# A gated recurrence with a highway layer: long GpSimd pieces and a new written-out order

## The chip, the cores and the metric

The kernel runs on one core of a Trainium2 chip. The metric is device time in microseconds (us) of one execution. The engines are TensorE (PE in the profile), VectorE (DVE), ScalarE (ACT), GpSimd (POOL) and SyncE (SP), whose queue issues all large DMAs here.

## The reference

Four sequences of 6,336 tokens with 256 channels pass a gated linear recurrence, and its output passes a highway layer. Cut to what is computed:

```python
sig = 1.0 / (1.0 + np.exp(-f_logit))
f = lower_bound + (1.0 - lower_bound) * sig
i = 1.0 - f
for t in range(S):                       # per sequence
    h = f[:, t] * h + i[:, t] * x[:, t]
    y[:, t] = h
x = y.reshape(B * S, D)
H = np.maximum(x @ w_h, 0.0)
T = 1.0 / (1.0 + np.exp(-(x @ w_t + b_t)))
out = T * H + (1.0 - T) * x
```

x, f_logit and the output are float32, 25,344 x 256 each, 26 MB; the kernel reads two of them and writes one.

## The kernel before, in words

The tokens are cut into 28 units (`units`): two of 256 tokens, one of 512, 23 of 1,024, one of 512 and one of 256. With P = 128 partitions, a unit of 1,024 tokens has NB = 8 blocks of 128. Every unit goes through the same steps, each a small function `do_<letter>`:

- `l`, `x`: SP loads f_logit and x of the unit (1 MB each for 1,024 tokens), each into one of six slots (L263).
- `u`: ACT takes the sigmoid of -f_logit (L275), tokens on partitions.
- `b`: u * x, in float16 x float32 to bfloat16 (L283). It is cut into quarters of 512 columns (two blocks); POOL does them, or DVE where the token ends in `v`.
- `i`, `p`: PE transposes u and b into PSUM (L289, L309), one instruction group for each half of the channels. `p` needs all quarters of its unit's b.
- `f`: the gate from the transposed u (L300 on ACT; L298 on DVE with `v`).
- `s`: the recurrence itself, `tensor_tensor_scan` on DVE (L326), one for each half; the carry ties each unit to the one before.
- `z`, `g`: the two matrix products (`ffn`, L343, and L141 for the repeated weights).
- `t`: sigmoid of z on ACT (L356). `d`: DVE, max(-(1-lower_bound) y, g), that is H - x (L360).
- `E`, `e`: the product d * t (`times`, L365), 2,048 columns for a unit of 1,024 tokens, four quarters. `E` does quarters on POOL, one of up to 512 columns at a time, up to the column that the unit's last number gives; `e` does the rest on DVE in one instruction.
- `o`: PE adds y and e, and so transposes them back (L384, L385); half a unit at a time. `c`: ACT (or DVE with `v`) copies it from PSUM (L394, L392) into one of four slots o. `w`: SP writes it (L399).

Nothing is scheduled at run time. The string `order` is the program: its tokens, read from left to right, are issued one by one, and each engine keeps that order. A token is a letter, the unit, after a dot the half or quarter, and after a colon the slot of the buffer that it fills (`b5.2:2` is quarter 2 of b of unit 5, into slot 2; `*k` adds k filling matmuls). SP's queue is in order too: a `w` that waits for its `c` keeps back the `l` and `x` behind it.

Two things tie POOL to DVE. `shared` remembers the last DVE instruction that takes two inputs from SBUF (b, e, a few at the start) and makes the next POOL instruction wait for it:

```python
        if not gpsimd:
            held[:] = [ins]
        elif held:
            tc.add_manual_dep(ins.ins, held.pop().ins.name, ...
```

And both feed the same consumers: `o` needs all quarters of e that lie in its tokens, whichever engine made them.

Of the kernel before, what the change touches and what calls it, by code (L numbers as in the profile page):

```python
# [19 lines left out]
def kernel(  # L20
# [20 lines left out]

    units = [
        (0, 128, 2, 0, 'y', 4, 512),
        (0, 128, 2, 256, 'y', 4, 512),
        (0, 128, 4, 512, 'y', 4, 1024),
        (0, 128, 8, 1024, 'y', 4, 512),
        (0, 128, 8, 2048, 'y', 4, 0),
        (0, 128, 8, 3072, 'y', 4, 2048),
        (0, 128, 8, 4096, 'y', 4, 2048),
        (0, 128, 8, 5120, 'y', 4, 0),  # L50
        (0, 128, 8, 6144, 'y', 4, 512),
        (0, 128, 8, 7168, 'y', 4, 1536),
        (0, 128, 8, 8192, 'y', 4, 512),
        (0, 128, 8, 9216, 'y', 4, 2048),
        (0, 128, 8, 10240, 'y', 4, 256),
        (0, 128, 8, 11264, 'y', 4, 2048),
        (0, 128, 8, 12288, 'y', 4, 2048),
        (0, 128, 8, 13312, 'y', 4, 1024),
        (0, 128, 8, 14336, 'y', 4, 0),
        (0, 128, 8, 15360, 'y', 4, 2048),  # L60
        (0, 128, 8, 16384, 'y', 4, 0),
        (0, 128, 8, 17408, 'y', 4, 2048),
        (0, 128, 8, 18432, 'y', 4, 1024),
        (0, 128, 8, 19456, 'y', 4, 1024),
        (0, 128, 8, 20480, 'y', 4, 2048),
        (0, 128, 8, 21504, 'y', 4, 1024),
        (0, 128, 8, 22528, 'y', 4, 1024),
        (0, 128, 8, 23552, 'y', 4, 512),
        (0, 128, 4, 24576, 'y', 4, 512),
        (0, 128, 2, 25088, 'y', 4, 0),  # L70
    ]
# [4 lines left out]
z0.1:1 d1.0:1 f3.1:3 z0.0:2 i3.0:0 d1.1 s2.0:2 p2.1:1 t0.1:0 b3.3v x5:5 t0.0 z1.1:0 s2.1 l6:1 g2.0*4:1 b3.1 b3.0v
f3.0:2 u4:2 x6:0 z1.0:2 E0.0:0 b4.2:1 b4.1 t1.0:1 b4.0 p3.1:0 t1.1 i4.1:1 b4.3 f4.1:1 o0.0:2 g2.1:0 d2.0:2 z2.1:1
s3.1:3 p3.0:1 c0.0:0 z2.0:2 w0.0 d2.1 t2.1:2 l8:2 i4.0:0 E1.0:1 t2.0 f4.0:0 x7:1 E2.1:2 E2.0 s3.0 p4.1:0 z3.1:1 u5:0
s4.1:0 p4.0:1 b5.2:2 g3.0:0 t3.1:0 s4.0 b5.1 i5.1:0 d3.0:0 u7:1 g3.1:1 f5.1:3 u6:2 i7.1:1 i5.0:0 g4.1:2 f7.1:2 d3.1
g4.0:0 o2.0:1 f5.0:1 c2.0:1 d4.1:2 b5.0 b5.3 l9:3 w2.0 p5.0:1 z3.0:2 b6.0:0 b6.3 p5.1:0 b6.2 x8:2 b6.1 t3.0 o1.0:2  # L80
z4.0:1 u8:0 d4.0 x9:3 z4.1:0 s5.0:2 s5.1 t4.0:1 i6.0:1 E3.0:0 b7.1:1 c1.0v:2 w1.0 t4.1 e3 e4:2 i6.1:0 b7.0 f6.0:0
g5.1:1 z5.0:0 p6.1:1 l10:4 f6.1:1 p6.0:0 u9:2 d5.1:1 o3.0:2 c3.0:3 o4.0:1 b7.2 g5.0:2 c4.0:0 s6.1:1 b7.3 b8.0:2 i8.1:1
w3.0 w4.0 z5.1:1 t5.0:2 o3.1:0 b8.2 f8.1:3 s6.0 d5.0 t5.1 p7.1:1 i7.0:0 c3.1:1 b9.1:0 b9.0 E5.1:1 o4.1:2 s7.1:3 g6.0:1
f7.0:1 c4.1:2 d6.0:0 p7.0:0 E5.0 i8.0:1 z6.1:0 s7.0 u10:1 z6.0:1 g6.1:2 b8.3 l12:5 f8.0:0 b8.1 E5.3 E5.2 w3.1 w4.1
i9.0:1 p8.0:0 b9.3 b9.2 d6.1 o5.1:2 s8.0:0 t6.1:0 t6.0 f9.0:2 g7.0:1 i9.1:1 E6.3:0 c5.1:3 p8.1:0 x10:4 E6.2 z7.0:0
l11:0 E6.1 d7.0:2 o5.0:2 f9.1:1 g7.1:1 u12:0 s8.1 c5.0:0 p9.1:1 d7.1 i10.1:0 t7.0:1 f10.1:0 z8.0:2 z7.1:1 b10.0:1
b10.1 g8.1:0 p9.0:0 t8.0:2 z8.1:2 t7.1 s9.1:2 d8.1:1 u11:2 g8.0:1 w5.1 i12.1:1 E6.0 t8.1 b10.2 s9.0 x11:5 b10.3
f12.1:3 o6.1:0 e7:2 x12:0 d8.0 o6.0:2 i11.1:1 w5.0 p10.1:0 b11.3:2 z9.0:1 c6.1:1 f11.1:1 e8:1 b12.3:0 i10.0:1 g9.0:0
l13:1 c6.0:2 s10.1:1 t9.0:0 b11.1 b11.0 l15:2 b12.0 z9.1:2 f10.0:2 p10.0:0 o7.1:1 w6.1 i11.0:1 t9.1 g9.1:2 c7.1:3
d9.0:0 s10.0 o7.0:1 d9.1 f11.0:0 b11.2 p11.0:0 w6.0 b12.2 u13:1 s11.0:3 E9.1:0 x13:1 z10.1:2 E9.0 c7.0:0 e9 t10.1:1  # L90
g10.1:0 w7.1 i13.1:1 d10.1:2 b12.1 p11.1:0 s11.1 u15:2 g10.0:2 E9.2 o9.1:1 o9.0:0 f13.1:2 x15:2 E8.0 l14:3 b13.0:1
i12.0:1 b13.2 c9.1:1 w7.0 b13.3 i15.1:0 z11.0:1 b15.1:2 f12.0:0 p12.0:1 d10.0 z10.0:2 c9.0:2 x14:3 t11.0:0 o8.0:0
f15.1v:1 t10.0 w9.0 p12.1:0 b13.1 o8.1:2 s12.0:2 g11.1:1 c8.0:3 s12.1 i13.0:1 u14:0 E10.0:2 z12.1:0 b15.0 w9.1 d11.1:0
p13.1:0 z11.1:1 f13.0:0 i14.1:1 c8.1:0 e10 b14.1:0 w8.0 s13.1:0 g11.0:2 b14.2 t12.1:2 t11.1 l16:4 z12.0:0 b14.3
f14.1:3 w8.1 b14.0 x16:4 g12.0:1 t12.0 i14.0:0 p13.0:1 f14.0:2 d11.0 o10.0:2 d12.0:1 o10.1:1 c10.0:2 s13.0 l17:5
g12.1:0 E11.2:0 E11.0 E11.1 i15.0:1 p14.1:0 d12.1 c10.1:1 u16:1 z13.0:2 g13.0:0 e12:1 t13.0:1 f15.0:0 s14.1:1 o11.0:1
c11.0:3 E11.3 z13.1:2 p14.0:1 b16.3:1 b15.2 t13.1 b15.3 i16.0:0 f16.0:3 o11.1:1 d13.0:2 b16.0 g13.1:2 i16.1:0 w10.1
s14.0 c11.1:0 w10.0 p15.1:1 l20:0 d13.1 u17:0 w11.0 x17:5 b16.1 E12.0 s15.1:3 f16.1:2 z14.1:1 z14.0:0 b16.2 g14.1:2
d14.1:0 p15.0:1 l19:1 w11.1 i17.1:0 t14.1:0 E13.2:2 E13.3 s15.0 o12.1:2 E13.1 t14.0 g14.0:0 l18:2 x19:0 x18:1 u20:2
o12.0:1 c12.1:1 w12.1 d14.0 E13.0 p16.0:1 z15.0:2 b17.1:0 l21:3 f17.1:1 b17.0 b17.3 c12.0:2 E14.2:0 p16.1:0 t15.0:2  # L100
b17.2 s16.0:2 o13.1:1 g15.0:0 E14.1 i17.0:1 u19:1 o13.0:2 s16.1 f17.0:0 d15.0:1 p17.0:0 s17.0:0 g16.0:0 c13.0:3
c13.1:0 p17.1:1 u18:0 z15.1:1 E14.0 z16.1:2 E14.3 d16.0:2 i19.1:0 s17.1 g16.1:0 t15.1 w12.0 w13.0 x21:3 g15.1:1 d15.1
f19.1:3 w13.1 i18.0:0 i20.0:1 b19.1:2 b19.3 t16.1:1 g17.0:2 x20:2 b18.2:1 f18.0:2 i18.1:0 o14.0:1 b18.0 d16.1 d17.0:0
b18.3 b18.1 e15:1 E15.1 g17.1:0 o14.1:2 d17.1 b19.2 E15.0 f20.0:0 f18.1:1 c14.0:1 p18.1:1 u21:0 z16.0:1 z17.0:0
s18.1:1 t16.0 p18.0:0 o15.1:1 t17.0:0 b19.0 s18.0 b21.2:0 o15.0:0 c14.1:2 p19.1:1 z17.1:2 c15.1:3 e16:2 E17.1:0
b20.1:1 c15.0:0 i19.0:0 z18.1:1 b20.0 b20.3 l22:4 t17.1 b20.2 w14.0 g18.0:0 f19.0:1 z18.0:2 w14.1 p19.0:0 s19.1:3
E17.3 i20.1:1 d18.0:1 w15.1 t18.1:2 t18.0 o16.1:1 E17.0 g18.1:2 o16.0:0 b21.1 s19.0 d18.1 f20.1:2 w15.0 p20.0:1
i21.1:0 c16.1:1 z19.0:1 c16.0:2 E17.2 f21.1:3 x22:4 g19.1:0 b21.0 u22:1 b21.3 s20.0:2 z19.1:2 p20.1:0 i22.0:1 d19.1:2
s20.1 l23:5 t19.0:1 g19.0:0 o17.0:1 i21.0:0 f22.0:1 w16.1 t19.1 e18:1 g20.1:2 c17.0:3 f21.0:0 w16.0 d19.0 p21.0:1
o17.1:1 b22.1:2 b22.3 E19.1:2 d20.1:0 u23:2 p21.1:0 E19.2 z20.0:0 s21.0:0 o18.0:2 c17.1:0 t20.0:0 b22.0 z20.1:1  # L110
i23.1:1 x23:5 s21.1 b22.2 g20.0:0 c18.0:1 t20.1 o18.1:2 f23.1:2 d20.0 l24:0 p22.0:0 c18.1:2 w17.0 s22.0:1 i22.1:1
g21.0:1 z21.1:0 f22.1:0 i23.0:1 u24:0 b23.2:1 b23.1 p22.1:0 z21.0:2 d21.0:1 t21.1:2 E19.3 s22.1 g21.1:1 b23.0 E19.0
w17.1 o19.0:0 t21.0 E20.1:0 w18.0 f23.0:3 b23.3 x24:1 d21.1 c19.0:3 l25:1 o19.1:2 p23.0:1 i24.0:0 w18.1 z22.0:1 e20
c19.1:0 s23.0:3 b24.0:0 f24.0:1 g22.1:0 g22.0:2 E20.0 i24.1:1 x25:0 d22.1:2 b24.2 t22.0:1 p23.1:0 o20.1:1 d22.0 u25:1
b24.1 z22.1:0 b24.3 w19.0 s23.1 f24.1:0 w19.1 E21.0:1 l26:2 e21 o20.0:2 b25.0:2 l27:3 c20.1:1 p24.1:1 t22.1 b25.1
g23.1:1 c20.0:2 s24.1:2 i25.0:0 b25.3 z23.0:0 f25.0:3 z23.1:2 E21.1 i25.1:0 w20.1 b25.2 p24.0:1 t23.0:0 g23.0:0 t23.1
d23.1:0 o21.0:2 E22.0:2 w20.0 o21.1:1 E22.2 f25.1:2 c21.0:3 s24.0 E22.1 p25.0:0 x27:2 d23.0 c21.1:0 z24.0:2 x26:3
E22.3 z24.1:1 u26:2 s25.0:0 g24.1:0 p25.1:1 t24.0:2 d24.1:1 s25.1 t24.1 i26.0:0 f26.0:0 o22.0:2 o22.1:1 E23.0:0
g24.0:0 i26.1:0 b26.1:1 c22.0:1 b26.0 c22.1:2 d24.0 u27:0 z25.0:2 i27.0:1 e23 e24:1 g25.0:1 f26.1:1 z25.1:0 d25.0:2
w21.0 t25.0:1 E24.0 p26.1:0 o23.0:2 f27.0:3 E24.1 p26.0:1 o24.0:1 t25.1 w22.0 g25.1:0 c23.0:3 w21.1 b27.0:0 s26.1:1  # L120
# [319 lines left out]
```

## Time and profile before

| | |
|---|---|
| three timed runs | 210.14, 210.24, 210.43 us; median 210.24 |
| span of the profiled execution, first to last instruction | 208.8 us |
| what the runs' median has beside that span | 1.4 us (the page gives no time of the execution other than its span) |
| busy: PE, DVE, ACT, POOL | 192.3, 194.4, 195.0, 171.7 us |
| moved by DMA | 78.69 MB, mean 377 GB/s |
| granted TensorE clock | 0.994 |
| b on POOL, 512 columns | 96 instructions, mean 1,179 ns |
| E on POOL, 512 columns | 54, mean 1,168 ns; one of 256 columns, 677 ns |
| e on DVE | 17, from 512 to 2,048 columns, 459 to 1,208 ns |

In the page, a busy time is the sum of the engine's instructions with overlaps counted once. On DVE, ACT and POOL the next instruction usually starts before the recorded end of the one ahead, so the distance between two starts in a dense stretch says what an instruction costs its engine, and it is shorter than the recorded duration. The rows with 40 digits cut the span into slices of 5.2 us; a digit is the busy share in tenths.

### The profile page before, as it was taken

The page shows a single profiled execution, that of the slowest core. Times are in us where ns is not written, and L with a number is a line of the kernel's source. Part 1 is how long each engine was busy: PE and PEld are TensorE (multiplying, and loading weights), DVE is VectorE, ACT ScalarE, POOL GpSimd, SP SyncE. Part 2 cuts the span into 40 slices and gives each one's busy share as a digit, 9 for nine tenths or more (in the row PEclk, how much of TensorE's full clock was granted, in tenths as well). Part 3 has the DMA queues.
Part 4 walks back from the last instruction along what each step waited for, and adds up shares of the span by engine and source line. Part 5 has one row for each costly group of instructions (what it writes and reads, how often), then busy time and mean ns, then how long its engine had stood idle before and what let it go on. Part 6 is the DMA issues. An engine that isn't in the chain of part 4 may idle for free.

```text
span 208.8 us, 4668 instructions
## 1 busy us (share of the span) xinstructions
PE 192.3 (92%) x1827; PEld 132.6 (64%) x1827; DVE 194.4 (93%) x154; ACT 195.0 (93%) x191; POOL 171.7 (82%) x162
## 2 busy tenths in 40 slices
...
DVE  0799998999999999999999999999999999999970
...
DMA  5999999999999999999999999999998999926676
GB/s 230 391 427 414 416 422 424 414 410 425 415 426 409 419 399 336 392 417 317 425 413 403 417 416 421 432 408 421 421 428 350 342 372 400 333 110 257 248 296 258
DMA packets 15982, 78.69 MB, mean 377 GB/s; under 512 B 1748, under 2 KB 2264, under 8 KB 10072
## 3 DMA queue, kind: packets, MB, share of 16 engines
...
## 4 chain that ended last, share of the span: by engine, by line
PE 44%; DMA 17%; DVE 15%; ACT 12%; issue 5%; POOL 3%; SPq 2%; ACTq 0%; DVEq 0%; POOLq 0%
DMA l<-in_f_logit_dram 13%; DVE y L326 9%; PE op L385 6%; PE z L343 6%; PE op L384 6%; PE g L343 6%; PE z L141 5%; PE bT L309 5%; PE uT L289 5%; PE g L141 5%; DVE d L360 4%; ACT f L300 4%; DMA x<-in_x_dram 4%; ACT o L394 3%; ACT u L275 2%
## 5 line engine op out<-in xcount | busy, mean ns | idle before, releaser
L283 POOL TENSOR_TENSOR bv<-u,x 128x512 bf16<-128x512 f16 x96 | 110.3, 1179 | 21.7 <-DMA x<-in_x_dram 9.6
L326 DVE TENSOR_TENSOR_SCAN y<-f,y,bT 128x1024 bf16<-128x1024 f16 (+5 forms) x54 | 106.7, 1991 | 1.1 <-ACT f L300 0.5
L365 POOL TENSOR_TENSOR e<-d,t 128x512 bf16<-128x512 bf16 (+1 forms) x55 | 62.5, 1159 | 7.6 <-DVE e L365 4.5
L360 DVE SCALAR_TENSOR_TENSOR d<-y,ncc,g 128x1024 bf16<-128x1024 bf16 (+2 forms) x56 | 63.0, 1140 | 1.1 <-PE g L343 0.9
L300 ACT ACTIVATE f<-uT,ncc 128x1024 f16<-128x1024 f16 (+2 forms) x53 | 56.4, 1073 | 3.0 <-PE uT L289 2.9
L356 ACT ACTIVATE t<-z,bt 128x1024 bf16<-128x1024 f32 (+2 forms) x56 | 57.2, 1060 | 0.6 <-PE z L141 0.2
L394 ACT COPY o<-op 128x1024 f32<-128x1024 f32 (+1 forms) x50 | 50.7, 1038 | 2.2 <-PE op L385 1.4
L275 ACT ACTIVATE u<-l 128x2048 f16<-128x2048 f32 (+2 forms) x28 | 48.8, 1748 | 2.9 <-DMA l<-in_f_logit_dram 2.9
L384 PE MATMUL op<-diag,y 128*128 128x128 f16 x396 | 49.4, 219 | 1.9 <-ACT t L356 1.3
L385 PE MATMUL op<-ident_b,e 128*128 128x128 bf16 x396 | 49.3, 219 | 0.8 <-DVE e L365 0.6
L385 PEld LDWEIGHTS <-e 128*128 128x128 bf16 x396 | 44.0, 113 | 6.4 <-issue 2.9
L384 PEld LDWEIGHTS <-y 128*128 128x128 bf16 x396 | 44.2, 113 | 2.3
L343 PE MATMUL g<-y,w_sb 128*128 128x512 bf16 (+1 forms) x112 | 39.2, 367 | 0.8 <-DVE d L360 0.4
L343 PE MATMUL z<-y,w_sb 128*128 128x512 bf16 (+1 forms) x112 | 39.0, 367 | 0.4 <-DVE d L360 0.4
L309 PE MATMUL bT<-ident_f,bv 128*128 128x128 f32 x198 | 32.0, 279 | 4.2 <-ACT f L300 2.4
L141 PE MATMUL g<-y,w_sb 128*128 128x512 bf16 x92 | 34.9, 379 | 0.0
L141 PE MATMUL z<-y,w_sb 128*128 128x512 bf16 x92 | 34.9, 379 | 0.0
L289 PEld LDWEIGHTS <-u 128*128 128x128 f16 x396 | 26.1, 98 | 12.3 <-issue 3.7
L289 PE MATMUL uT<-ident_h,u 128*128 128x128 f16 x396 | 30.6, 219 | 2.7 <-DVE y L326 2.0
L343 PEld LDWEIGHTS <-w_sb 128*128 128x128 f16 x224 | 21.8, 98 | 15.8 <-issue 0.4
L309 PEld LDWEIGHTS bT<-ident_f,bv 128*128 128x128 f32 x198 | 22.2, 141 | 12.6 <-DVE y L326 3.1
L141 PEld LDWEIGHTS <-w_sb 128*128 128x128 f16 x184 | 18.0, 98 | 16.7 <-issue 2.1
...
## 6 DMA issues: line engine op xcount, KB each, us to landing
...
l<-in_f_logit_dram SPq DMA_DIRECT2D x23, 1024.0 KB, 11.3
x<-in_x_dram SPq DMA_DIRECT2D x23, 1024.0 KB, 10.1
...
```

The source lines that it names most:

```text
L141: return pe.add_instruction(mybir.InstMatmult(name=nc.get_next_instruction_name(), start_tensor_calc=start, stop_tensor_calc=stop, tile_si ...
L283: shared(pin(e.tensor_mul(st[n]["bv"][:, k].rearrange("p d j -> p j d"), st[n]["u"][:, q:q + 2], st[n]["x"][:, q:q + 2])), not eng)
L289: pin(nc.tensor.transpose(uT[:, j * P:(j + 1) * P], st[n]["u"][:, j, h * P:(h + 1) * P], ident_h))
L300: pin(nc.scalar.activation(to, of, AF.Identity, scale=ncc[:, h:h + 1], bias=1.0))
L309: pin(nc.tensor.transpose(words[:, k:k + g * (P - 1) + 1:g], pair, ident_f))
L326: pin(nc.vector.tensor_tensor_scan(y[:, c:e], st[n]["f", h][:, c:e], st[n]["bT", h][:, c:e], 0.0 if fresh else carry[h], op0=ALU.mult, op1 ...
L343: pin(nc.tensor.matmul(p[:, a:e], w, half(n, "y", ki)[:, a:e], start=ki == 0, stop=ki == NH - 1))
L356: pin(nc.scalar.activation(half(n, "t", m), st[n]["z", m][:, :tokens(n)], AF.Sigmoid, bias=bt[:, m:m + 1]))
L360: pin(nc.vector.scalar_tensor_tensor(half(n, "d", m), half(n, "y", m), ncc[:, m:m + 1], st[n]["g", m][:, :tokens(n)], op0=ALU.mult, op1=AL ...
L365: shared(pin(eng.tensor_mul(st[n]["e"][:, a:e], st[n]["d"][:, a:e], st[n]["t"][:, a:e])), eng is nc.gpsimd)
L384: pin(nc.tensor.matmul(o, half(n, "y", h)[:, cols], diag[:, h], start=True, stop=False))
L385: pin(nc.tensor.matmul(o, half(n, "e", h)[:, cols], ident_b, start=False, stop=True))
```

## The change

The functions for b, E and e take a range of quarters instead of one: `b5.0-4` is one instruction over quarters 0 to 3 of b, 2,048 columns, and `E3.3-4` is quarter 3 of e on POOL. `e` on DVE takes a range as well. The column at which POOL's share of e ends is no longer a number of the unit, and two unused fields of a unit go. The new list gives POOL 70 quarters of e in 31 instructions (before, 54.5 in 55) and 98 quarters of b in 32 (96 in 96). DVE keeps 29 quarters of e in 11 instructions (44.5 in 17) and one quarter of b (three). Four f of 1,024 columns are on DVE (one, and one of 512); no c is on DVE (one of 512 columns). Units, buffers, slots and every other instruction are the same in kind and number; their order on each engine and the slots that they take are new.

```diff
-    units = [
-        (0, 128, 2, 0, 'y', 4, 512),
...
+    units = [
+        (0, 2), (256, 2), (512, 4), (1024, 8), (2048, 8), (3072, 8), (4096, 8), (5120, 8),
...
     order = """
+l0:0 l3:1 pc:0 wh u0:0 i0.0:0 i0.1:1 k*10 l1:2 x0:0 wt cc dg f0.1v:0 f0.0:1 x1:1 u3:1 u1:2 i1.0*5:0 WH b0.0-1v:0 l2:3
+x2:2 f1.0:2 p0.1*2:1 b1.0-1:1 i1.1:0 x3:3 l4:4 s0.1:0 p0.0:1 s0.0 f1.1:3 p1.1*2:0 p1.0:1 g0.0:1 s1.1:1 u2:0 b2.0-2:2
+i2.1:0 s1.0 i2.0:1 g1.1:0 b3.0-4:0 d0.0:0 x4:4 g1.0:2 g0.1:1 f2.1:0 d1.1:1 WTa i3.1:0 d1.0 z1.1:0 z0.0:2 f2.0:1
+p2.0*1:1 f3.1:3 t0.0:0 d0.1 z0.1:1 t0.1 p2.1:0 z1.0:2 l5:5 s2.0:2 s2.1 i3.0:1 f3.0v:2 g2.0*4:1 t1.1:1 u4:2 z2.1:0
+d2.0:2 E0.0-1:0 t2.1:2 t1.0 l7:0 p3.1:0 i4.1:1 b4.0-4:1 x5:5 o0.0:1 g2.1:0 s3.1:3 l6:1 f4.1:1 z2.0:2 c0.0:0 p3.0:1
+x6:0 w0.0 t2.0 d2.1 i4.0:0 s3.0 f4.0:0 u5:0 E1.0-1:1 u7:1 p4.1:0 p4.0:1 z3.0:1 g3.1:2 z3.1:0 s4.1:0 t3.0:0 s4.0
+E2.0-2:2 i5.0:0 t3.1 d3.1:0 g3.0:1 d3.0 f5.0:3 i5.1:1 f5.1:2 g4.0:0 u6:2 i7.1:0 o2.0:2 b5.0-4:2 p5.1:1 o1.0:1 f7.1:1
+d4.0:1 E3.3-4:0 z4.1:0 c1.0:1 l8:2 s5.1:2 t4.1:1 x7:1 c2.0:2 p5.0:0 z4.0:1 E3.0-3 i6.0:1 s5.0 t4.0 g4.1:0 g5.1:2
+i6.1:0 b6.0-4:0 x9:2 b7.3-4:1 o3.1:1 w1.0 x8:3 u8:0 f6.0v:0 i8.1:1 f6.1:2 d4.1 z5.0:0 d5.1:2 l9:3 c3.1:3 p6.0:0
+e4.0-4:2 o3.0:2 f8.1:3 p6.1:1 w2.0 o4.1:1 t5.0:2 z5.1:0 s6.0:1 s6.1 i7.0:0 l10:4 c3.0:0 c4.1:1 g5.0:2 o4.0:1 t5.1
+f7.0:0 x10:4 w4.1 b7.0-3 u9:2 p7.0:1 d5.0 g6.0:0 c4.0:2 w4.0 z6.1:2 i8.0:0 f8.0:2 s7.0:3 t6.1:0 b8.0-4:2 p7.1:1 i9.0:0
...
+f10.0:0 z9.0:2 u15:1 b11.0-4:2 p10.1:1 p10.0:0 s10.1:1 z9.1:1 t9.1:0 o7.1:0 l13:2 s10.0 g9.1:1 b12.0-4:0 w5.1 t9.0
+i11.0:1 x13:1 c7.1:1 g10.0:2 d9.1 f11.0:2 i12.0:0 o7.0:0 w6.1 d10.0:1 p11.0:1 z10.1:1 e9.0-4:1 x14:3 u13:2 s11.0:3
+f12.0:0 z10.0:2 p11.1:0 t10.1:1 s11.1 w7.1 g10.1:1 l14:3 E8.0-4:0 t10.0 i13.1:1 d10.1 c7.0:2 w6.0 o9.1:2 o9.0:0
...
+g13.0:2 t13.1:1 l19:0 t12.1 b15.0-4:0 d13.0:1 g12.0:1 i16.1:1 p14.0:0 d12.0 u17:0 s14.0 f16.1:3 z13.0:0 g13.1:2
+o11.0:1 E12.2-4:0 t13.0 e12.0-2 i16.0:1 p15.0:0 o11.1:0 d13.1 c11.0:2 o12.0:1 f16.0:2 b16.3-4:1 g14.1:2 s15.0:3
...
+i20.0:1 w13.0 i18.0:0 g17.1:1 d16.0 f20.0:2 i18.1:1 f18.0:1 o14.1:0 f18.1:0 b18.0-4:0 d15.1 g17.0:2 w13.1 w12.1
+c14.1:0 d17.1:0 p18.1:0 o14.0:1 E15.2-3 u21:0 x20:3 E15.3-4 o15.0:0 c15.0:1 b19.0-4:1 p18.0:1 d17.0 s18.1:1 w14.1
+z16.0:2 t16.0 i19.0:0 s18.0 o15.1:0 c14.0:3 e16.0-4:2 z17.0:2 x21:2 b20.0-4:2 p19.0:1 f19.0:0 c15.1:2 t17.0:0 z17.1:1
+p19.1:0 s19.0:3 o16.1:0 z18.0:2 t17.1 i20.1:1 s19.1 c16.1:0 w15.0 l22:4 g18.1:1 o16.0:0 E17.0-3:1 w14.0 d18.1:2
...
+o17.0:2 u22:1 c17.0:3 i21.0:1 b21.0-4:0 w15.1 s20.1 t18.1 x22:4 g18.0:1 g19.1:2 i22.0:0 E19.0-1:0 f21.0:3 d18.0 w16.0
+o17.1:0 d19.1 e18.1-4:2 w17.0 g20.1:1 f22.0:2 p21.0:1 c17.1:2 p21.1:0 z19.1:2 u23:2 d20.1:0 x23:5 l24:0 o18.1:0
...
+s23.1 i24.1:0 z22.0:0 f24.1:3 o20.0:2 x26:3 o20.1:1 t22.0 c20.0:1 w20.0 e21.0-4:2 i25.0:0 b25.1-2:1 p24.0:1 g23.0:0
...
+w21.0 E22.0-2:0 t24.0:2 E22.2-4 z24.1:1 d24.1:2 f26.1:2 p25.1:0 o22.0:2 o22.1:0 i27.0:1 t24.1 s25.1 E23.0-4:1 g24.0:1
+c22.0:2 f27.0:3 d24.0 c22.1:1 i26.0:1 w21.1 f26.0:0 g25.0:2 z25.0:0 z25.1:1 b26.0-2:2 d25.0:1 p26.1:0 e24.0-4:2
+o23.0:2 p26.0:1 t25.0:1 o24.0:0 b27.0-1:0 t25.1 s26.1:1 g25.1:1 w22.0 c23.0:0 E25.0-2:0 s26.0 i27.1:0 c24.0:2 f27.1:1
+w20.1 o24.1:2 p27.1:1 d25.1 c24.1:3 s27.1:2 p27.0:0 z26.1:0 w22.1 E25.3-4 o23.1:1 s27.0 t26.1:0 w23.0 c23.1:1 g26.0:2
+o25.1:0 d26.0:0 g26.1:1 z26.0:2 w24.0 w24.1 c25.1:0 t26.0 e25.2-3 d26.1 z27.0:1 e26.1-2:2 z27.1:1 o25.0:0 e26.0-1
+w23.1 t27.1:2 t27.0 c25.0:2 g27.0:0 g27.1:0 d27.1:2 o26.0:1 c26.0:3 d27.0 e27.0-1:1 w25.1 w25.0 o27.0:2 c27.0:1 w26.0
+w27.0
...
-    def do_b(n, k, eng, slot):
+    def do_b(n, k, eng, slot, end):
         if "bv" not in st[n]:
             st[n]["bv"] = sb([P, NB // 2, D, 2], BF16, "bv", slot)
-        q = 2 * k
+        blk = slice(2 * k, 2 * end)
         e = nc.vector if eng else nc.gpsimd
-        shared(pin(e.tensor_mul(st[n]["bv"][:, k].rearrange("p d j -> p j d"), st[n]["u"][:, q:q + 2],
-                                st[n]["x"][:, q:q + 2])), not eng)
+        shared(pin(e.tensor_mul(st[n]["bv"][:, k:end].rearrange("p k d j -> p k j d"),
+                                st[n]["u"][:, blk].rearrange("p (k j) d -> p k j d", j=2),
+                                st[n]["x"][:, blk].rearrange("p (k j) d -> p k j d", j=2))), not eng)
...
-    def do_E(n, k, eng, slot):
-        times(n, nc.gpsimd, k * 512, min(units[n][6], k * 512 + 512), slot)
-
-    def do_e(n, k, eng, slot):
-        times(n, nc.vector, units[n][6], NH * tokens(n), slot)
+    def do_E(n, k, eng, slot, end):
+        times(n, nc.gpsimd, k * 512, end * 512, slot)
+
+    def do_e(n, k, eng, slot, end):
+        times(n, nc.vector, k * 512, end * 512, slot)
...
         n, _, k = name[1:].partition(".")
-        here["do_" + name[0]](int(n), int(k or 0), token.endswith("v"), slot)
+        k, _, end = k.partition("-")
+        span = (int(end),) if end else ()
+        here["do_" + name[0]](int(n), int(k or 0), token.endswith("v"), slot, *span)
```

More of the change, by code (lines that the diff above doesn't have):

```diff
@@ L42 @@
     units = [
-        (0, 128, 2, 0, 'y', 4, 512),
[L44 to L66, printed above, removed]
@@ L76 @@
[L76 to L85, printed above, removed]
@@ L86 @@
[L86 to L120, printed above, removed]
@@ L121 @@
-w22.1 i27.1:0 c24.0:1 o24.1:2 s26.0 p27.0:1 f27.1:2 d25.1 w23.0 p27.1:0 E23.1 z26.1:1 s27.0:2 w24.0 E25.0:2 c24.1:0
-o23.1:0 z26.0:2 s27.1 t26.1:2 c23.1:2 z27.1:1 z27.0 e25 g26.0:1 w24.1 d26.0:1 t26.0 o25.1:0 w23.1 E26.0:1 t27.1:0
-g26.1:2 d26.1 c25.1:3 o25.0:1 w25.1 c25.0:1 g27.0:0 g27.1 e26 w25.0 d27.1:0 t27.0 o26.0:0 d27.0 c26.0:0 e27:0 o27.0:1
-w26.0 c27.0:2 w27.0
+l0:0 l3:1 pc:0 wh u0:0 i0.0:0 i0.1:1 k*10 l1:2 x0:0 wt cc dg f0.1v:0 f0.0:1 x1:1 u3:1 u1:2 i1.0*5:0 WH b0.0-1v:0 l2:3
+x2:2 f1.0:2 p0.1*2:1 b1.0-1:1 i1.1:0 x3:3 l4:4 s0.1:0 p0.0:1 s0.0 f1.1:3 p1.1*2:0 p1.0:1 g0.0:1 s1.1:1 u2:0 b2.0-2:2
@@ new lines @@
+f12.0:0 z10.0:2 p11.1:0 t10.1:1 s11.1 w7.1 g10.1:1 l14:3 E8.0-4:0 t10.0 i13.1:1 d10.1 c7.0:2 w6.0 o9.1:2 o9.0:0
+f13.1:2 c9.1:0 p12.0:1 i15.1:0 w7.0 z11.1:2 b13.0-4:1 l16:4 c9.0:1 g11.1:1 w9.0 f15.1:1 E10.0-4:2 i13.0:0 s12.0:2
+t11.1:0 f13.0:0 u14:0 p12.1:1 o8.1:0 d11.1:0 s12.1 p13.1:0 o8.0:2 w9.1 c8.0:3 c8.1:2 z11.0:1 i14.1:1 o10.0:2 t11.0
+x15:2 g11.0:0 s13.1:0 p13.0:0 l17:5 f14.1v:3 i14.0:1 d11.0 o10.1:1 s13.0 g12.1:0 u16:2 c10.0:1 b14.0-4:2 w8.1 z12.0:2
+f14.0:2 d12.1:2 i15.0:1 E11.1-4:1 p14.1:0 E11.0-1 x16:4 s14.1:1 c10.1:0 w8.0 z13.1:1 z12.1:0 t12.0:2 w10.0 f15.0:0
@@ new lines @@
+g13.0:2 t13.1:1 l19:0 t12.1 b15.0-4:0 d13.0:1 g12.0:1 i16.1:1 p14.0:0 d12.0 u17:0 s14.0 f16.1:3 z13.0:0 g13.1:2
+o11.0:1 E12.2-4:0 t13.0 e12.0-2 i16.0:1 p15.0:0 o11.1:0 d13.1 c11.0:2 o12.0:1 f16.0:2 b16.3-4:1 g14.1:2 s15.0:3
+c11.1:3 c12.0:1 u19:1 x17:5 d14.1:0 z14.1:0 p15.1:1 s15.1 z14.0:1 t14.1:0 w11.0 b16.0-3 g14.0:2 t14.0 E13.0-4:2
+i17.1:0 o12.1:0 l20:1 w12.0 p16.1:1 w11.1 f17.1:0 z15.0:1 p16.0:0 d14.0 s16.1:2 o13.0:2 c12.1:2 t15.0:2 l18:2 g15.0:0
+u20:2 s16.0 c13.0:1 i17.0:1 d15.0:2 o13.1:1 b17.0-4:2 p17.0:0 f17.0:1 z15.1:2 z16.1:0 c13.1:3 s17.0:0 E14.0-4:1
```

37 lines of the change are left out of this document (21 added, 16 removed), and 3 rows, old and new, of the table units.

## The prediction

> **What bounds the kernel now.** I read the page first, then the windows, the timelines of VectorE (DVE), ScalarE (ACT) and GpSimd (POOL), and the groups by form.
>
> The page's busy rows and slices:
>
> ```profile
> span 208.8 us, 4668 instructions
> PE 192.3 (92%) x1827; PEld 132.6 (64%) x1827; DVE 194.4 (93%) x154; ACT 195.0 (93%) x191; POOL 171.7 (82%) x162
> DVE  0799998999999999999999999999999999999970
> DMA  5999999999999999999999999999998999926676
> GB/s 230 391 427 414 416 422 424 414 410 425 415 426 409 419 399 336 392 417 317 425 413 403 417 416 421 432 408 421 421 428 350 342 372 400 333 110 257 248 296 258
> ```
>
> No engine stands out, and DMA runs near 415 GB/s until about 160 us, with dips near 80 and 96 us. The windows show who waits in the middle:
>
> ```profile
> core 0: us, PE busy (x) PEld busy (x) DVE busy (x) ACT busy (x) POOL busy (x), PEclk, DMA share, GB/s
> ...
> 120.00:140.00 20.00, 19.31 (x191) 13.64 (x189) 20.00 (x14) 20.00 (x19) 18.49 (x17) 1.00 1.01 419
> ```
>
> DVE and ACT have no free time. Durations overlap, so I priced work by start-to-start distances in dense stretches: scan y of 1,024 columns 2.26 us, d 1.17, ACT's f and t 1.00, u 1.81, o 0.90. By these, DVE has 191.6 us of work, and of its 12.1 us of idle time only 3.2 lie after its e4 at 41.2 us. ACT has 189.0 us of work and about 6.4 us of idle time between 20 us and 199 us. PE's instructions do not change, and in its timeline a 1,024-token unit takes only some 7.0 us of dense work against about 7.6 us of span (per unit: uT and bT 0.9 each, z and g 1.7 each, op 1.8), so PE gives about 15 us of room. So DVE bounds the kernel, with ACT close behind.
>
> POOL looks free at 82%, and is not. Wherever DVE does e or b (two SBUF inputs), `shared` makes the next POOL instruction wait, and the timelines (start, us, instruction) of POOL, then of DVE, show the other direction too:
>
> ```profile
> 128.55 4.56 POOL L283 TENSOR_TENSOR bv<-u,x 128x512 bf16<-128x512 f16 x4 [0.21 <-ACT f L300]
> 133.73 1.16 POOL L365 TENSOR_TENSOR e<-d,t 128x512 bf16<-128x512 bf16 x1 [0.62 <-DVE e L365]
> ```
>
> ```profile
> 132.68 0.97 DVE L365 TENSOR_TENSOR e<-d,t 128x1024 bf16<-128x1024 bf16 x1
> ...
> 169.07 0.69 DVE L365 TENSOR_TENSOR e<-d,t 128x1024 bf16<-128x1024 bf16 x1
> ```
>
> The e at 132.68 met a POOL piece that ran to 133.11 and took 0.97 us instead of 0.69: it got through only when that piece was over. So POOL and DVE's two-input work share one resource, "the port". Its work is 168.8 us (POOL) + 13.3 (e on DVE) + 1.9 (b on DVE) = 184.0 us, and from the first b at 9.9 us to E26's end at 201.7 there are 191.8 us. It is nearly as full as DVE.
>
> **The change, part by part.**
>
> *Price of a long POOL piece.* The trace has no piece over 512 columns. It has one of 256:
>
> ```profile
> L365 POOL TENSOR_TENSOR e<-d,t 128x512 bf16<-128x512 bf16 x54 | 61.8, 1168 | 7.6 <-DVE e L365 4.5 <-DVE d L360 2.4 <-DVE bv L283 0.7
> L365 POOL TENSOR_TENSOR e<-d,t 128x256 bf16<-128x256 bf16 x1 | 0.7, 677 | 0.0
> ```
>
> Start to start these are 1.115 and 0.63 us: 1.90 ns a column and 0.14 us an instruction (b's 512 takes 1.125, so 0.15). A 2,048-column piece then costs 4.03 to 4.05 us; the other end is four short pieces, 4.46 to 4.50. I take the fit, nearest to both rows, and keep the other end for a rival.
>
> The Trainium skill, "GPSIMD Engine Reference", section "Elementwise — side-by-side cycle accounting", gives 2.6 cycles an element and 4,497 ns for 2,048 fp32 columns of such an add, which is 2.2 ns a column and leaves merging nothing to save; the 256-column row (0.63 us where half of 1.115 would be 0.56) speaks against that here, for these types, and by it the sum below would come out some 13 us later.
>
> *POOL.* E goes from 54.5 to 70 quarters and b from 96 to 98: 17.5 quarters x 0.97 = +17.0 us. Instructions go from 55 to 31 (E) and 96 to 32 (b): -24 x 0.14 - 64 x 0.15 = -13.2. Together +3.8.
>
> *DVE.* e before: 4 of 2,048 columns at 1.12, one of 1,792 at 1.01, 4 of 1,536 at 0.87, 5 of 1,024 at 0.60, 3 of 512 at 0.45 = 13.3 us. After: 5, 0, 1, 1 and 4 of these = 8.9. Two b fewer: -1.3. The c on DVE goes to ACT: -0.6. f: three of 1,024 more at 1.22, one of 512 fewer at 0.66: +3.0. Sum -3.3.
>
> *ACT.* Three f of 1,024 fewer: -3.0; one f of 512 (0.57) and one c of 512 (0.56) more. Sum -1.9.
>
> *Port.* +3.8 - 4.4 - 1.3 = -1.9. PE and DMA bytes: 0.
>
> *The order.* DVE's e in the middle are fewer: e4, e9, e12, e16, e18, e21, e24 instead of thirteen from e4 to e24. By the prices above, the work that the new list puts between these meetings is, on DVE, 36.7, 27.6, 29.2, 15.0, 21.4 and 16.0 us (sum 145.9), and on the port 36.8, 27.6, 29.3, 14.5, 21.3 and 15.8 (145.3). The two go in step, with 0.1 us to spare at a meeting. In the old list, from e4 to e24, the same difference was 2.5 us over twelve steps, 0.2 each. A meeting's handshake shows as 0.2 to 0.4 us of POOL idle beyond e itself (1.27 before E11.3 for an e of 1.01). Six meetings fewer at about 0.15 that reaches DVE, against 0.1 less to spare at six: I leave DVE's idle time as it was.
>
> *The sum.* The first loads come in the same order, so x5 lands as before and POOL's b5 starts at 28.69 us. Then b5 4.05, E3.3 1.12, E3.0-3 3.06, b6 4.05, b7.3 1.13: e4 can start at 42.1, where it started at 41.2. From e4 to e27's end DVE has 155.8 us of work (before 159.3). With the 3.2 us of idle time: 42.1 + 155.8 + 3.2 = 201.1, where the trace has 203.7. From there to the end of the span 5.1 us passed (op, c27, the last write): 206.2. ACT must end 2.5 us earlier with 1.9 less work, so 0.6 of its 6.4 us of idle time must go. The last POOL piece, E25.3, ends at 42.1 + 150.8 of port work + 6 x 0.38 = 195.2, and c25.1 needs it by about 196: hidden, with under 1 us of cover. The runs last 1.4 us longer than the span (median 210.24 against 208.8): **207.7 us**.
>
> *Writes* move behind loads on SP's queue: w10.1, w6.0 and w18.0 stand several loads later. o has four slots, and a write's landing must beat the next c in its slot; the tightest in the middle is w15.0 to c16.0, 6 us, with one load ahead, where before w14.0 took 11 us to land, just when c16.1 started. No cost taken, up to 1 us if it misses.
>
> **Rivals.**
>
> *The port becomes the bound (slower).* The saving per merged start rests on one 256-column row; b has no second size at all. From b5 on 97 starts are merged away. All the cover is under 1 us, and the gain 2.6: if a merged start saves 0.11 us or less instead of 0.15, POOL is late for s and for E25.3 by the whole gain. At a third of the saving lost, 97 x 0.05 = 4.9 us, less 1 of cover: 211.6 us. At nothing saved, some 221. For it: the port has nothing to spare. Against it: the fit needs an error of 40 ns, and the 512-column distances vary by 8 ns.
>
> *DVE is held by a whole piece (slower).* Before, no piece in front of a DVE e was longer than 1.2 us, and the longest hold was 0.28. In the new list e9, e16 and e21 stand behind pieces of 4.05 us. If POOL lags before each, and DVE waits half the added length, 1.4 us, three times: 207.7 + 4.2 = 211.9. It decides from a lag of about 0.9 us at each, since 3 x 0.9 eats the gain. Against it: work between meetings is equal to 0.1 us, so a lag once paid need not come again.
>
> The Trainium skill, "SBUF — State Buffer", section "Who interferes with whom", says that the pair of ports shared by VectorE and GpSimd is an exclusive lock and that the second to issue blocks fully until the first is done; the row of 0.97 us agrees, for a hold of 0.28 us, and no run here shows one behind a 4 us piece.
>
> *DMA holds the gain back.* Between 100 and 155 us the queue is full: x18 landed at 128.39 and its b started at 128.55. The new list wants 50.9 MB landed (l21) when u21 starts, about 131.5; at the old supply, 49.3 MB by 128.39 and 415 GB/s, they are there at 132.2. If the dips at 80 and 96 us stay, about 1 us of the gain goes: 208.7.
>
> *It does nothing.* Long pieces bring what more e on POOL costs, and DVE's gain turns into waits for b: 210.2.
>
> **How the numbers follow.** Forecast 0.50, for 207.7 (its own range 206.0 to 208.6: DVE's idle time between 1.6 and 4.1 us). DMA 0.12 (208.7). Port 0.24 (from 210.7 upwards, 211.6 as its middle). Held DVE 0.08 (211.9). Nothing 0.06. This measurement tells 0.2% (0.42 us) from no change. Faster: 0.50 + 0.11 = 0.61; same 0.06 (with a little of DMA, less a little of nothing); slower 0.33. The range 206.0 to 212.0 leaves out the far half of the port case and the few hundredths below.
>
> **What would show it.** Right: POOL's 2,048-column groups at 4.03 to 4.10 us start to start, DVE work about 188.4 us, e4 at about 42.1, e27's end at about 201, DVE's e of 2,048 columns still near 1.2 us. Port wrong: those pieces at 4.2 or more, and scans y or transposes bT waiting for POOL's bv. Held DVE: single e of 2 us and more. DMA: u waiting for l between 115 and 150 us, and dips in GB/s near 80 and 96 us as before. ACT's o waiting for out_dram: the writes were moved too far.

## The result, and the profile after

Four timed runs of the changed kernel took 207.60, 207.71, 207.90 and 208.35 us, median 207.81; the kernel before, on the same chip, 210.26. The ratio is 0.988 (0.985 to 0.991): faster by 2.4 us, where 207.7 us was forecast. The profiled execution's span is 205.9 us (before 208.8), so the runs' median lies 1.9 us beyond it. Beside its own span every run on record, of either kernel, takes 1.7 to 1.9 us more; the execution on the page of before was some 0.3 us longer than the median one, whose span is 208.5. All times below are medians of all executions of a kernel; in the runs at 247.53 and 227.01 us two and one of six executions were in a slower state, and the others have medians of 246.38 and 226.85.

From the page of the kernel after, the rows shown of before:

```profile
span 205.9 us, 4570 instructions
PE 191.5 (93%) x1827; PEld 132.6 (64%) x1827; DVE 191.0 (93%) x147; ACT 192.5 (93%) x190; POOL 175.7 (85%) x74
DVE  0779999999999999999999999999999999999970
DMA  6999999999999999999999999999999997886686
GB/s 228 384 427 415 420 417 423 411 417 425 403 416 420 426 419 423 412 394 406 411 424 366 406 377 413 426 414 391 415 369 338 422 424 303 290 326 239 264 318 258
```

DVE lost 3.4 us of busy time and ACT 2.5, POOL gained 4.0. The second thing to see is in the last row: the old dips at the 16th figure (336 GB/s, about 80 us) and the 19th (317, about 96 us) are gone; the same places now show 423 and 406. Smaller ones have come at the 22nd and 24th (366 and 377).

The stretch from 120 to 140 us in the windows of after:

```profile
core 0: us, PE busy (x) PEld busy (x) DVE busy (x) ACT busy (x) POOL busy (x), PEclk, DMA share, GB/s
120.00:140.00 20.00, 19.11 (x186) 13.50 (x187) 19.73 (x13) 19.45 (x19) 18.69 (x8) 1.00 1.01 407
```

Nothing has become slack: DVE, ACT, POOL and DMA are all close to full. The groups by form of after (busy us, mean ns):

```profile
L255 POOL TENSOR_TENSOR bv<-u,x 128x2048 bf16<-128x2048 f16 x19 | 78.5, 4136 | 2.9 <-DMA x<-in_x_dram 1.6 <-DVE e L338 1.3
L338 POOL TENSOR_TENSOR e<-d,t 128x2048 bf16<-128x2048 bf16 x8 | 32.7, 4091 | 1.2 <-DVE e L338 1.2
L338 POOL TENSOR_TENSOR e<-d,t 128x512 bf16<-128x512 bf16 x12 | 13.9, 1166 | 1.5 <-PE bT L282 1.1 <-DVE d L333 0.4
L338 DVE TENSOR_TENSOR e<-d,t 128x2048 bf16<-128x2048 bf16 x5 | 6.7, 1334 | 0.0
```

A piece of 2,048 columns takes 4.1 us recorded, less than four times 1,166 ns. DVE's e of 2,048 columns has a mean of 1,334 ns where it was 1,208 before: it waits a little for POOL, as the timelines of DVE and, below, POOL show.

```profile
41.70 1.58 DVE L338 TENSOR_TENSOR e<-d,t 128x2048 bf16<-128x2048 bf16 x1
...
78.96 1.41 DVE L338 TENSOR_TENSOR e<-d,t 128x2048 bf16<-128x2048 bf16 x1
...
200.70 0.42 DVE L338 TENSOR_TENSOR e<-d,t 128x512 bf16<-128x512 bf16 x1
```

```profile
36.95 5.27 POOL L255 TENSOR_TENSOR bv<-u,x 128x2048 bf16<-128x2048 f16 x2
```

e4 starts at 41.70 but gets through only after POOL's b7.3, which ends at 36.95 + 5.27 = 42.22. The last e ends at 201.12.

### The profile page after: what moved, and what is told of

It reads as the page before. It is cut to its first block, busy times and chain, and to the rows that moved or that the text cites. A ratio compares the mean times of both kernels' runs of the same rounds, so it can differ in the third digit from the quotient of the medians.

```text
span 205.9 us, 4570 instructions
## 1 busy us (share of the span) xinstructions
PE 191.5 (93%) x1827; PEld 132.6 (64%) x1827; DVE 191.0 (93%) x147; ACT 192.5 (93%) x190; POOL 175.7 (85%) x74
## 4 chain that ended last, share of the span: by engine, by line
PE 41%; DMA 16%; ACT 15%; issue 10%; DVE 10%; POOL 5%; SPq 1%; ACTq 0%; DVEq 0%; POOLq 0%
DMA l<-in_f_logit_dram 8%; DVE y L299 6%; PE op L358 6%; PE op L357 6%; PE g L316 5%; PE bT L282 5%; PE z L316 5%; DMA x<-in_x_dram 5%; PE z L113 5%; PE g L113 5%; PE uT L262 4%; ACT o L367 4%; ACT t L329 4%; ACT f L273 4%; ACT u L247 3%
## 5 line engine op out<-in xcount | busy, mean ns | idle before, releaser
L255 POOL TENSOR_TENSOR bv<-u,x 128x2048 bf16<-128x2048 f16 (+3 forms) x32 | 102.3, 3211 | 16.8 <-DMA x<-in_x_dram 10.7
L338 POOL TENSOR_TENSOR e<-d,t 128x512 bf16<-128x512 bf16 (+3 forms) x31 | 73.6, 2391 | 2.7 <-DVE e L338 1.2
L273 ACT ACTIVATE f<-uT,ncc 128x1024 f16<-128x1024 f16 (+2 forms) x51 | 53.8, 1070 | 3.3 <-PE uT L262 3.2
L367 ACT COPY o<-op 128x1024 f32<-128x1024 f32 (+1 forms) x51 | 51.8, 1039 | 1.5 <-PE op L358 1.3
L262 PEld LDWEIGHTS <-u 128*128 128x128 f16 x396 | 26.3, 98 | 12.0 <-issue 3.8
L262 PE MATMUL uT<-ident_h,u 128*128 128x128 f16 x396 | 31.3, 220 | 2.0 <-DVE y L299 1.2
```

What stands on the lines that cost most here:

```text
L255: shared(pin(e.tensor_mul(st[n]["bv"][:, k:end].rearrange("p k d j -> p k j d"), st[n]["u"][:, blk].rearrange("p (k j) d -> p k j d", j=2) ...
L262: pin(nc.tensor.transpose(uT[:, j * P:(j + 1) * P], st[n]["u"][:, j, h * P:(h + 1) * P], ident_h))
L273: pin(nc.scalar.activation(to, of, AF.Identity, scale=ncc[:, h:h + 1], bias=1.0))
L338: shared(pin(eng.tensor_mul(st[n]["e"][:, a:e], st[n]["d"][:, a:e], st[n]["t"][:, a:e])), eng is nc.gpsimd)
```

## The theories

- P (pieces and room on the port): long pieces save about 0.145 us of port time for each start that is merged away; that room pays for the e that leave DVE.
- O (order of loads and writes): the new list gives the loads a longer lead on SP's queue, and that carries the gain, or part of it.
- Q, formed on the way: the lead carries nothing by itself, but the faster order can't run without it. SP sits at a write until its copy is made; if the loads issued ahead of it run out meanwhile, DMA stands still.

The kernel before took 210.24 to 210.37 us beside every group of runs, so the experiments are compared by their medians with after's 207.8, and with before by the ratio and its interval.

## Experiments on the pieces and the port

**The changed kernel again.**

> The changed kernel once more, beside the kernel before on the same chip, so that the others have a yardstick. Both theories: 207.6 to 208.2 us, 0.986 to 0.991 of before. P (pieces): long POOL pieces give room on the port that POOL and VectorE share, and that room lets VectorE and ScalarE give work away. O (order): the gain comes from the new order alone, above all from loads that no longer stand behind writes; the length of the pieces is by the way.

208.03 us, ratio 0.9894 (0.988 to 0.9909). So after stands at 207.8 to 208.0.

**Short pieces in the new list.** Every product on POOL is cut back to 512 columns, 168 instead of 63; nothing else changes.

```diff
-b5.0-4:2
+b5.0-1:2 b5.1-2 b5.2-3 b5.3-4
```

> The new list, but every b and E on POOL is issued in pieces of 512 columns again, one behind the other (168 instructions instead of 63). P: 105 more starts at 0.145 us are 15.2 us more on the port, of which some 14 lie behind b5 and about 1 is covered: 219 to 222 us, with VectorE's y and PE's bT waiting for bv. O: the order is the same, so 207.6 to 208.5 us.

220.48 us, ratio 1.0491 (1.0472 to 1.0509): P's figure. 12.7 us for 105 more starts are 0.12 us each. SP's order is that of after, so O alone is out. The timeline of DVE and that of POOL in this kernel (the products are at L345 and L262) show how the lost room reaches DVE:

```profile
79.10 5.49 DVE L345 TENSOR_TENSOR e<-d,t 128x2048 bf16<-128x2048 bf16 x1
```

```profile
74.46 9.05 POOL L262 TENSOR_TENSOR bv<-u,x 128x512 bf16<-128x512 f16 x8
```

POOL is late with the eight pieces that stand before e9 in the list; they end at 83.51, and DVE's product, issued at 79.10, ends at 84.59. It got in between no two of them, although three began after its own start.

**Pieces of 1,024 columns.** 97 products on POOL instead of 63.

```diff
-b5.0-4:2
+b5.0-2:2 b5.2-4
```

> After's list with POOL's pieces held to 1,024 columns: 97 POOL products instead of 63. P: a start costs 0.145 us; 34 more are 4.9 us of port work, of which under 1 us is covered: 211 to 213 us, about a third of the way to the 220.5 us that 105 more starts took. If only very short pieces cost something, or the cost is in the order: 207.6 to 209.0.

211.90 us, ratio 1.0078 (1.0065 to 1.0091): within P's range. 4.1 us for 34 starts are again 0.12 each, so the price goes with the number of starts. Where it lands is read from the groups by form of this kernel, DVE's products:

```profile
L340 DVE TENSOR_TENSOR e<-d,t 128x2048 bf16<-128x2048 bf16 x5 | 9.6, 1914 | 0.0
L340 DVE TENSOR_TENSOR e<-d,t 128x512 bf16<-128x512 bf16 x4 | 1.7, 424 | 0.2
L340 DVE TENSOR_TENSOR e<-d,t 128x1024 bf16<-128x1024 bf16 x1 | 1.6, 1599 | 0.0
L340 DVE TENSOR_TENSOR e<-d,t 128x1536 bf16<-128x1536 bf16 x1 | 1.3, 1257 | 0.0
```

Together 14.2 us; the same eleven products take 6.7 + 1.7 + 0.9 + 0.8 = 10.1 in after. So DVE's products take 4.1 us longer, waiting for the port, and the kernel loses 4.1 us. With pieces of 512 columns the same products take 19.5 us, 9.4 of the 12.7 us lost; most of the rest shows as idle time before scans.

**Merging alone.** The old list with its old shares; POOL's adjacent pieces become one (100 products on POOL instead of 151), nothing else moves.

```diff
-b4.2:1 b4.1 b4.0 b4.3
+b4.0-4:1
```

> The old list with the old shares of work, but POOL pieces that already stood next to each other are one instruction (100 instead of 151). P: 51 starts x 0.145 = 7.4 us of port time come free, but VectorE keeps 191.6 us of work and ScalarE 189.0, so only what VectorE lost at meetings can come back: 209.2 to 210.2 us. O: the old order stays, 210.0 to 210.5. A third theory, that merging alone brings the gain: 207.5 to 208.5.

211.13 us, ratio 1.0046 (1.0032 to 1.0059): a miss for every expectation. The timeline of DVE has both sides:

```profile
132.56 0.68 DVE L342 TENSOR_TENSOR e<-d,t 128x1024 bf16<-128x1024 bf16 x1
...
196.19 1.28 DVE L337 SCALAR_TENSOR_TENSOR d<-y,ncc,g 128x1024 bf16<-128x1024 bf16 x1 [0.65 <-PE g L117]
```

The hold of before is gone (0.68 us instead of 0.97), and by 191 us DVE is 0.4 us ahead. But at 196 us a d waits 0.65 us for PE, which in before it did not, and DVE ends 0.5 us behind. PE's timeline shows why it is late:

```profile
194.26 0.25 PE L362 MATMUL op<-ident_b,e 128*128 128x128 bf16 x1 [0.51 <-POOL e L342]
```

It waits for a product of 1,024 columns on POOL, from 192.07 to 194.20 us, which before came in two pieces, the first of them done by 193.6. A merged piece hands over its first columns only at its end, a price that neither the prediction nor the expectation had. Room on the port brought nothing to a list that doesn't spend it.

**Spending less of it.** E13 and E20 go back to DVE: DVE +2.3 us of work, the port -5.9.

```diff
-E13.0-4:2
+e13.0-4:2
-E20.0-4:1
+e20.0-4:1
```

> The new kernel with e of units 13 and 20 on VectorE instead of POOL, at the same places of the list: VectorE 2.3 us more work, the port 5.9 us less. If VectorE binds: 209.8 to 211.0 us (2.3, and up to 1 more where VectorE meets a piece). If the port alone binds: 206.0 to 207.8 us.

209.65 us, ratio 0.9968 (0.9958 to 0.9978). 1.6 to 1.8 us later than after for 2.3 us of work on DVE, just under the range for "DVE binds"; of the 5.9 us freed on the port at most 0.7 come back.

**Spending more of it.** The upper half of e21 goes to POOL.

```diff
-e21.0-4:2
+E21.2-4:2 e21.0-2
```

> After's list with the upper half of e21 on GpSimd (E21, 1,024 columns) and the lower half on VectorE. VectorE's work falls by 1.12 - 0.60 = 0.5 us, POOL's grows by 2.1 and the port's by 1.6. If VectorE and ScalarE bind and the port has room of 2 us and more: 207.2 to 208.0, a gain of at most 0.5. If the port is as full as the prediction had it (under 1 us of cover): 208.4 to 209.6.

208.98 us, ratio 0.9933 (0.9921 to 0.9945), 1.2 us later than after. The timeline of DVE:

```profile
173.28 0.69 DVE L338 TENSOR_TENSOR e<-d,t 128x1024 bf16<-128x1024 bf16 x1
174.50 2.35 DVE L299 TENSOR_TENSOR_SCAN y<-f,y,bT 128x1024 bf16<-128x1024 f16 x1 [0.54 <-ACT t L329]
189.78 1.95 DVE L338 TENSOR_TENSOR e<-d,t 128x2048 bf16<-128x2048 bf16 x1
```

e21 takes 0.52 us less than in after (1.21), but that is lost at once: the scan behind it waits 0.54 us and starts at 174.50, in after at 174.53; in both PE has just made a bT (at 174.41 and 174.44). Then e24 takes 1.95 us instead of 1.22, held by a POOL that is late. The port has under 1 us to spare here, as the prediction had it.

**The f shift undone.** Four f of 1,024 columns go back to ACT.

```diff
-f3.0v:2
+f3.0:2
```

(and the same for f6.0, f12.1 and f14.1)

> The new kernel with its four f of 1,024 columns on VectorE (f3.0, f6.0, f12.1, f14.1) given back to ScalarE: VectorE 4.7 us less work, ScalarE 4.0 us more. If both bound, as the prediction has it, ScalarE's 191.1 us of work end 1 to 4 us later: 208.9 to 211.9 us. If VectorE alone binds: 204 to 206.5 us.

211.01 us, ratio 1.0047 (1.0025 to 1.0069), some 3 us later than after although DVE has 4.7 us less to do. ACT binds as DVE does.

**How long POOL holds DVE.** After the kernel's work five rungs are added: a POOL product of 2,048 columns, 1, 3, 5, 7 or 9 short DVE steps of one SBUF input, then a DVE product of 512 columns with two.

> The new kernel, then five rungs at its end: a POOL piece of 2,048 columns starts together with 1, 3, 5, 7 or 9 VectorE instructions of 0.39 us that do not need the port, and then VectorE takes a product of 512 columns with two inputs from SBUF (0.42 us alone). The same product is computed again into e25, so the output stays what it is. If a held instruction waits for the whole piece: about 3.7, 2.9, 2.2, 1.4 and 0.7 us. If the port is shared between the two while both run: 0.4 to 0.9 us on each rung. The time itself is of no interest (about 250 us).

The DVE product took 3.85, 2.82, 1.79, 0.76 and 0.42 us. First and last rung in the timeline of DVE, and the first in that of POOL:

```profile
206.50 3.85 DVE L398 TENSOR_TENSOR junk<-d,t 128x512 bf16<-128x512 bf16 x1
...
247.08 0.42 DVE L398 TENSOR_TENSOR junk<-d,t 128x512 bf16<-128x512 bf16 x1
```

```profile
206.03 4.05 POOL L394 TENSOR_TENSOR e<-d,t 128x2048 bf16<-128x2048 bf16 x1 [0.59 <-DVE junk L392]
```

In four rungs DVE's product ends 0.27 to 0.29 us after POOL's, however early it began; in the fifth it begins after POOL's. POOL's takes 4.05 us in every rung. The steps took 0.52 us each where 0.39 had been expected, so the middle rungs came later than planned; the reading is the same. The Trainium skill, "SBUF — State Buffer", section "Who interferes with whom", calls these ports an exclusive lock on which the second to issue blocks fully; the 3.85 us agree, now for a whole long piece.

## Experiments on SP's queue

**Each write right behind its copy.**

```diff
-c2.0:2 ... x9:2 ... x8:3 ... l9:3 ... w2.0
+c2.0:2 w2.0 ... x9:2 ... x8:3 ... l9:3
```

(so for w2.0; all writes alike)

> The new list, but each write stands on SP's queue right behind its copy; loads that stood ahead of a late write now stand behind it. P: loads still land before they are needed for the most part, 207.6 to 208.6 us. O: loads come late again and DMA shows dips as in the old list, 209.5 to 210.5 us.

231.35 us, ratio 1.0994 (1.0976 to 1.1012): both theories missed by more than 20 us. From the list of waits:

```profile
POOL bv L255 <- DMA x<-in_x_dram: 28.3, 11, 7.8
ACT u L247 <- DMA l<-in_f_logit_dram: 20.7, 14, 3.8
```

and from SP's own list of waits (a write waiting for its copy):

```profile
SPq L372 <- ACT o L367: 163.8, 48, 12.3
```

In after this is 125.1 us. SP's waiting costs nothing as long as the loads already issued keep DMA busy; here they don't. The granted TensorE clock fell too, to 0.967 in this profiled execution and to 0.951 and 0.976 in those of the next two runs (after: 0.995); what part of these three losses is TensorE's was not separated.

**The old sequence of loads and writes under the new list of work.** SP's queue has the tokens l, x and w as the kernel before has them.

```diff
-l8:2 x7:1 x9:2 w1.0 x8:3 l9:3 w2.0
+l8:2 x7:1 l9:3 w2.0 x8:2 x9:3 w1.0
```

> The new list on every engine but SP: its queue has the old list's sequence of loads and writes, with the old slots for l and x. P (room on the port): VectorE, ScalarE and the port have the same work, and the old sequence fed a kernel 1% slower: 207.8 to 208.6 us. O (the order of loads and writes carries the gain): the dips in DMA near 80 and 96 us are back and u and b wait for loads, 209.5 us or more.

247.53 us, ratio 1.1788 (1.1739 to 1.1837). O has the sign only. The list of waits:

```profile
ACT u L247 <- DMA l<-in_f_logit_dram: 20.2, 9, 6.5
POOL bv L255 <- DMA x<-in_x_dram: 19.1, 5, 8.5
```

The two lists want their units in different order, so this says that the sequences must fit, and nothing on what the new one brings.

**Writes no further behind than in before.** 20 writes go forward, so that none passes more loads behind its copy than in the kernel before: 36 loads passed in all instead of 84 (before 43).

```diff
-c1.0:1 l8:2 ... x7:1 ... x9:2 ... w1.0
+c1.0:1 w1.0 l8:2 ... x7:1 ... x9:2
```

(so for w1.0; others by one to six loads)

> After's kernel with one thing undone: 20 of the 52 writes are put forward on SP's queue so that none passes more loads behind its copy than it does in the kernel before. Over the list the writes then pass 36 loads instead of 84 (before: 43; right behind their copies, 0, took 231.35 us). Theory P (pieces and room on the port): 207.6 to 208.6 us, since a write's place costs nothing as the prediction had it, and u's waits for l after 20 us stay under 1 us. Theory O (the loads' lead on SP's queue carries part of the gain): the 41 loads that passed a write in the new list stand behind it again, dips in GB/s near 80 and 96 us come back, u waits for l or POOL for x by 1 us and more, 209.5 us or later.

227.01 us, ratio 1.0785 (1.0767 to 1.0803): far beyond P, and O's "or later" holds more than was meant. One write shows it. SP's timeline in this kernel, then in after (L372 is a write, L235 a load):

```profile
22.45 0.90 SPq L235 DMA_DIRECT2D x<-in_x_dram  x1
35.36 0.34 SPq L372 DMA_DIRECT2D out_dram<-o  x1
```

```profile
22.32 1.00 SPq L235 DMA_DIRECT2D l<-in_f_logit_dram  x1
23.40 0.86 SPq L235 DMA_DIRECT2D x<-in_x_dram  x2
35.38 0.34 SPq L372 DMA_DIRECT2D out_dram<-o  x1
```

Both wait at w1.0 until 35.4 us, when c1.0 is made. After has issued three more loads ahead of it. Without them this kernel moves 221 GB/s from 28 to 36 us. From this came Q.

**The step on the writes undone.** 18 of the 51 writes go forward, so that no more loads are issued ahead of each than in before (38 loads in all; three that stand right behind their copies keep one or two more).

```diff
-o3.1:1 w1.0 x8:3 ... l9:3 ... e4.0-4:2 ... w2.0
+o3.1:1 w1.0 w2.0 x8:3 ... l9:3 ... e4.0-4:2
```

> After's list with 18 of its 52 writes put forward on SP's queue, so that no more loads are issued ahead of each than in the kernel before (38 loads pass no write any more; the writes that the new list has earlier than the old one stay). This is the prediction's step on the writes, undone. Q, the theory formed after the run in which 20 writes were put forward and the time rose to 227.01 us: SP waits at a write's place until its copy is made, the loads issued ahead of it run out meanwhile, and DMA stands still. With the loads' lead of the old list, its dips near 80 and 96 us come back (about 2.3 us of supply in all): 208.5 to 211 us, with u waiting for l by 1 us and more in the middle. P, with a write's place costing nothing unless it is as early as there: 207.6 to 208.4.

212.62 us, ratio 1.0132 (1.0109 to 1.0154): 4.8 us later than after and 1.6 us beyond Q's range. The trace has what Q names: the page's last row has the dip near 96 us again (19th figure, 310 GB/s; after 406), though not the one near 80, and one l pays for it. ACT's timeline, then DVE's:

```profile
120.94 1.91 ACT L247 ACTIVATE u<-l 128x2048 f16<-128x2048 f32 x1 [1.87 <-DMA l<-in_f_logit_dram]
```

```profile
124.81 2.35 DVE L299 TENSOR_TENSOR_SCAN y<-f,y,bT 128x1024 bf16<-128x1024 f16 x1 [2.27 <-ACT f L273]
```

A u that is 1.87 us late makes its f late, and the scan waits 2.27 us. DVE's e starts give the account: e4 1.0 us later than in after, e12 0.8, e16 4.0, e24 4.8. Not all of this is the loads'. The page's clock row has TensorE slowed in two places:

```profile
PEclk9999979999999999999999988999999999999999
```

From about 26 us the granted clock is 0.5 for 3.4 us, before SP reaches the first write that was moved (not before 36.7 us; until then it issues what it issues in after): a d then waits 0.65 us for PE, and that makes e4 late. The second such stretch follows the late u, from about 125 us. Another execution of this kernel, at a granted clock of 1.0, took 212.62 us all the same, so the slow clock is not needed for the 4.8 us; where that execution loses its time is not on record.

## Why the prediction was right, point by point

- *Price of a long piece* (4.03 to 4.05 us): 4.04 start to start for e, 4.06 to 4.10 for b; 3.06 for 1,536 columns and 2.09 for 1,024 (e) lie on the same line. The two split runs confirm the start's price without any fit: 0.12 us each reaches the end, in two doses. The figure of the Trainium skill, "GPSIMD Engine Reference", section "Elementwise — side-by-side cycle accounting", 4,497 ns for 2,048 fp32 columns, does not hold for these types: 4.04 to 4.10 us were measured.
- *Engines' work*: forecast were -3.3 us for DVE and -1.9 for ACT. By start-to-start distances in both traces they are about -3.5 (an f of 1,024 columns costs DVE 1.18 us, not 1.22) and -2.0. POOL's +3.8 is mis-summed: its own terms, 24 x 0.14 + 64 x 0.15 = 13.0, give +4.0. By the distances of after, with b's long pieces at 4.08 us, it was +4.6, so the port got 1.1 us less work instead of 1.9.
- *The sum*: e4 can run at 42.1 (42.2), e27 ends at 201.1 (201.12), the tail takes 5.1 us (4.8), the span 206.2 (205.9). By the forecast's 155.8 us of work, DVE's idle time from e4's start at 41.70 is 3.6 us against 3.2: the hold of e4 itself (0.37) is the difference. The step from the span to the runs was mis-sized: 1.4 us came from a page whose execution was longer than the median one, and 1.9 was measured. The span that was 0.3 us too long hid it. The mechanism is right to some 0.5 us; that the total agrees to 0.1 us is luck.
- *Cover of the last piece*: E25.3 ended at 195.80 (forecast 195.2), 0.6 us later; just before it POOL waited 0.37 us for a d. The claim of "under 1 us" on the port stands: 1.6 us more port work cost 1.2.
- *Port rival*: it needed a start to save 0.11 us or less, and POOL's distances show that it saves 0.14. The split kernels are this rival made real, with DVE held as the way in which it acts, not scans waiting for bv.
- *Held DVE*: the holds in after are 0.37, 0.2 and almost nothing; the lag never came to 0.9 us. Its premise, that the length of a piece sets the hold, was half right. The lag sets it: one long piece holds DVE for what is left of it, and so do short ones back to back.
- *Writes*: this step was wrong. "No cost taken, up to 1 us if it misses" asked only whether a later write could hurt. ACT's o never waited for out_dram, so it did not; but the move bought the loads' lead: with 18 writes put back the kernel takes 4.8 us more. No bound below nothing was set. That the forecast came out right all the same is partly luck: its sum carried DVE's 3.2 us of idle time over from before, and nothing in it said why the loads would keep up.
- *DMA rival*: in after the dips near 80 and 96 us were gone, so it did not come true. Where the writes are put back, the dip near 96 us and a u that waits for l, at 121 us, lie where it had them. Its term was mis-sized: "about 1 us" was the lateness of one load at the old supply, while there one late u costs the scan 2.27 us, since the f behind it shifts too, and the whole kernel takes 4.8 us more, not all of it traced to the loads.

Which part of the gain belongs to which part of the change can't be added up. Undoing the pieces loses 4.1 or 12.7 us, the f shift about 3, the e shift in part 1.7, the writes' places 4.8, all but the e shift more than the whole gain of 2.4. Each is a condition of the others; merging alone in the old list gained nothing. The new list with old pieces and old shares, and the old list with the writes later, were not tried; so it stays open whether the old list would have gained from a longer lead. Why the writes at their old places cost more in the new list than in the old was not settled either; the sequence of the loads differs too.
